# Queries in 1 KB runs, turned on VectorE, with scores on 32-row tiles and gates on GpSimd

## The chip, the cores and the metric

The kernel runs on one core of one Trainium2 chip. The metric is the device time of one execution in microseconds. Below, PE is the matrix engine TensorE, PEld its weight loads, DVE is VectorE, ACT is ScalarE, POOL is GpSimd, and SP is the engine that here issues the stores.

## The reference, cut to what matters

The inputs `q`, `k` and `v` have the shape (8 batches, 8 heads, 576 tokens, 64). A first attention pools keys and values by 8 to 72 of each. Its output, 512 features per token, goes into four experts, each a causal attention with 64-wide heads; a gate picks two of the four per token.

```python
k_p = k.reshape(B, H, Sp, pool, D).mean(axis=3)          # pool = 8, Sp = 72; v_p the same
scores = scale * np.matmul(q, k_p.transpose(0, 1, 3, 2))
attn = softmax(scores);  x = (attn @ v_p), heads side by side   # (8, 576, 512)
...
logits = x @ w_gate                                       # 4 experts
topk, w = the two largest of logits, softmax over these two
for e in range(E):
    q, k, v = x @ wq[e], x @ wk[e], x @ wv[e]
    a = softmax(scale * q @ k.T, causal)
    out += (w of e where e is picked) * (a @ v @ wo[e])
```

## The kernel before, in words

All work of a batch b is cut into small steps, and one long string `SEQ` (L551) gives the order of the steps of all batches, written out by hand. Each token names a step, its batch, for products the PSUM bank, and by a trailing d that DVE, not ACT, evacuates it. A trailing c sets `cut`, so that `wide` splits a product of 128 output rows into four of 32. PE, ACT, DVE and POOL each run their instructions in this order. SP's stores follow the order of the program among themselves.

Loads: `load` (L109) issues the tokens `L_q`, `L_k` and `L_v` on POOL, as DMAs that turn float32 into bf16. A batch's queries come in six loads of 96 tokens, with one token to a partition, so each run in memory is one head's 64 numbers, 256 B. Keys and values come in three loads each with two tokens to a partition. There are three raw buffers of each kind (`NRAW`). `load_weights` (tokens `W`) issues the weights on POOL too, and `order_weights` (tokens `c`) copies them into the order that the products need.

The first attention: `PK` and `PV` pool keys and values by products with a constant matrix; `kc` and `vc` evacuate them. `KT` transposes the pooled keys on PE (four flips, 96 columns each, one per pair of heads), `kt` evacuates them into `kpT`. `Q` transposes the queries of a pair of heads on PE (six flips) and `r` evacuates them into `qT`. `Es` computes the scores, with the 72 pooled keys padded to 96 output rows: for each of four pairs of heads two products of 512 columns, which lie in different 64-row tiles of PE, and for the last 64 tokens (`E4`) two products of 64 columns per pair. `es` takes the exponential on ACT, out of two banks at a time. `Dn` sums the exponentials by products, `dn` and `dx` form the reciprocal by a logarithm and an exponential on ACT, `Ov` multiplies by the values, and `ov` normalises on DVE into `xT`.

The experts: `P` projects queries and keys (`p` evacuates into `qk`), `V` projects values and gate logits (`v`). `Sb` and `sb` compute scores and exponentials (`etb`); `am` masks the diagonal blocks on POOL (`a`). `gate` is done in ten small steps per batch: g0 an exponential on ACT, and on DVE g1 to g3 the second largest logit by maxima and minima (five operations), g4 the mask, g5 to g9 the two weights. `Bv` multiplies by the values; `bv` normalises in three steps: `bz` a reciprocal on DVE, `bg` its product with the gate on DVE, `b` the scaling into `osc` on DVE. `T` and `t` transpose into `oT`; `Y`, `y` and `z` apply the last weight and store the output, from eight buffers `ofin`. At the start and wherever data are late, `warm_up` (tokens `H`) issues products that nobody reads, 51 in all.

Copies run through one helper (L176), products through `mm` (L185), transposes through `flip` (L194), so many rows of the profile share a line and are told apart by their tiles.

Of the kernel before, what the change touches and what calls it, by code (L numbers as in the profile page):

```python
# [12 lines left out]
MINOP = mybir.AluOpType.min  # L13
MAXOP = mybir.AluOpType.max
ISGE = mybir.AluOpType.is_ge
ISLE = mybir.AluOpType.is_le
ISEQ = mybir.AluOpType.is_equal
# [4 lines left out]
def kernel(  # L22
# [34 lines left out]
    NQC = S // KR  # L57
# [16 lines left out]
    qraws = bufs(NRAW, [KR, NQC, H, D], BF16, "qraw")  # L74
    kraws = bufs(NRAW, [KR, 3, H, 2, D], BF16, "kraw")
    vraws = bufs(NRAW, [KR, 3, H, 2, D], BF16, "vraw")
    kps = bufs(2, [KR, H * D], BF16, "kp")
    kpTs = bufs(2, [128, NHP, KR], BF16, "kpT")
    vps = bufs(2, [KR, H, D], BF16, "vp")
    qTs = bufs(8, [128, S], BF16, "qT")  # L80
    etas = bufs(2, [KR, NHP, 2, S], BF16, "eta")
# [24 lines left out]
    wst = {nm: const.tile([128, E, 2, 2, HD], BF16, name=f"wst_{nm}") for nm in ("q", "k", "v")}  # L106
    wst_g = const.tile([128, 2, 2, E], BF16, name="wst_g")

    def load(b, nm, c):  # L109
        if nm == "q":  # L110
            dst = qraws[b % NRAW][:, c, :, :]
            src = q[b, :, KR * c : KR * (c + 1), :].rearrange("h p d -> p h d")
        else:
            raw, T = (kraws, k) if nm == "k" else (vraws, v)
            dst = raw[b % NRAW][:, c, :, :, :].rearrange("p h t d -> p h (t d)")
            src = T[b, :, 2 * KR * c : 2 * KR * (c + 1), :].rearrange("h (p t) d -> p h (t d)", t=2)
        nc.gpsimd.dma_start(out=dst, in_=src)  # L117


    def load_weights(i):  # L120
        if i < 3:
            dst = wst["qkv"[i]][:].rearrange("p e g t d -> p (e g) (t d)")
# [9 lines left out]
    def order_weights(i, dve):  # L132
# [4 lines left out]
        else:  # L137
            copy(dve, wvg[:, :, 0 : E * HD].rearrange("p fc (e d) -> p fc e d", e=E),
                 wst["v"][:].rearrange("p e g t d -> p (g t) e d"))
            copy(dve, wvg[:, :, E * HD : VG], wst_g[:].rearrange("p g t e -> p (g t) e"))  # L140

    def setup_consts(step):
# [9 lines left out]
        else:  # L152
# [5 lines left out]
            nc.vector.tensor_scalar_mul(out=poolv[:], in0=poolk[:], scalar1=DSC)  # L158

# [56 lines left out]
    def pool_pe(b, bank, raw, mat):  # L216
        for t in range(2):
            for c in range(3):
                mm(psum[32 * c : 32 * c + 32, bank, :], mat[:, :], raw[:, c, :, t, :],
                   start=(t == 0), stop=(t == 1))  # L220

    def PK(b, bank):
        pool_pe(b, bank, kraws[b % NRAW], poolk)

    def kc(b, bank, dve):
        copy(dve, kps[b % 2][:], psum[0:KR, bank, :])

    def PV(b, bank):
        pool_pe(b, bank, vraws[b % NRAW], poolv)
# [7 lines left out]
    def KT(b, bank):  # L237
        for hp in range(NHP):
            flip(half_bank(bank)[:, KR * hp : KR * hp + KR],
                 kps[b % 2][:, 128 * hp : 128 * hp + 128])  # L240

    def kt(b, bank, dve):
        copy(dve, kpTs[b % 2][:],
             half_bank(bank)[:, 0 : NHP * KR].rearrange("p (a n) -> p a n", a=NHP))

    def Q(b, bank, hp):
        for c in range(NQC):
            flip(half_bank(bank)[:, KR * c : KR * (c + 1)],
                 qraws[b % NRAW][:, c, 2 * hp : 2 * hp + 2, :].rearrange("p h d -> p (h d)"))

    def r(b, bank, dve, hp):
        copy(dve, qTs[4 * (b % 2) + hp][:], half_bank(bank)[:, 0:S])


    def Es(b, bank, hp):
        for i in range(NHP) if hp == NHP else [hp]:
            c0, n, at_ = (MAIN, TAIL, TAIL * i) if hp == NHP else (0, MAIN, 0)
            for hh in range(2):
                r0 = hh * D
                mm(psum[0:KR, bank + hh, at_ : at_ + n], kpTs[b % 2][r0 : r0 + D, i, :],  # L260
                   qTs[4 * (b % 2) + i][r0 : r0 + D, c0 : c0 + n])

    def es(b, bank, dve, hp):
        eta = etas[b % 2]
        if hp == NHP:
            for hh in range(2):
                nc.scalar.activation(
                    out=eta[:, :, hh, MAIN:S],
                    in_=psum[0:KR, bank + hh, 0 : NHP * TAIL].rearrange("p (a n) -> p a n", a=NHP),
                    func=EXP, scale=ATT_EXP_SCALE,  # L270
                )
        else:
            nc.scalar.activation(  # L273
                out=eta[:, hp, :, 0:MAIN], in_=psum[0:KR, bank : bank + 2, :],
# [3 lines left out]
    def heads(b, g, cols):  # L278
        for i in range(4):
            yield i, 4 * g + i, etas[b % 2][:, 2 * g + i // 2, i % 2, cols]  # L280

# [9 lines left out]

    def dn(b, bank, dve, g):
# [6 lines left out]

# [36 lines left out]
    def gate(b, step):  # L336
# [14 lines left out]
        elif step == 1:  # L351
            L2 = L.rearrange("p c (a b) -> p c a b", b=2)
            for nm, op in (("hi", MAXOP), ("lo", MINOP)):
                nc.vector.tensor_tensor(
                    out=tmp(nm, 2, 1), in0=L2[:, :, :, 0:1], in1=L2[:, :, :, 1:2], op=op
                )
        elif step == 2:
            for nm, src, op in (("s2", "hi", MINOP), ("s3", "lo", MAXOP)):
                nc.vector.tensor_tensor(
                    out=tmp(nm, 1), in0=got(src)[:, :, 0, :], in1=got(src)[:, :, 1, :], op=op  # L360
                )
        elif step == 3:
            nc.vector.tensor_tensor(
                out=tmp("m2", 1), in0=got("s2"), in1=got("s3"), op=MAXOP
            )
        elif step == 4:
            nc.vector.tensor_tensor(
                out=tmp("msk", E), in0=L, in1=got("m2").to_broadcast([128, n, E]), op=ISGE
            )
        elif step == 5:  # L370
            nc.vector.tensor_mul(out=tmp("W", E), in0=got("Ex"), in1=got("msk"))
        elif step == 6:
            nc.vector.tensor_add(
# [9 lines left out]
        else:  # L383
            nc.vector.tensor_mul(
# [91 lines left out]
    def bv(b, bank, step, ep, part):  # L476
# [6 lines left out]
        elif step == "bg":  # L483
            nc.vector.tensor_mul(
# [220 lines left out]
```

The softmax here doesn't subtract the row's maximum and nothing guards it: scores larger than these inputs give would overflow.

## Time and profile before

| What | Value |
|---|---|
| Median of 3 runs | 167.1 us (166.84 to 168.86) |
| Span of the profiled execution, first to last instruction | 165.0 us |
| Time of the profiled execution itself | not given apart from its span |
| Mean granted clock of PE | 0.996 |
| First product of an expert projection | 26.23 us |
| Last copy of an output ends, last stores are issued | 161.15 us, 161.22 us |
| Query transposes on PE | 192 |
| Loads of queries, keys, values | 48, 24, 24 |
| DMA packets, and those under 512 B | 84204, 79312 |

The page gives the span and the busy time of each engine. Groups of instructions have the line, the engine, the operation, the tiles by name (output, then inputs), the shape, the count, the busy time and the mean length of one. The timeline has the start and the length of each instruction or run of like instructions, and in brackets the idle time of the engine before it with what ended that. A product is pipelined: its length holds a passage through the array that overlaps the next product, so what it costs is read from start to start. The mean costs that the steps below meet most often are these:

| Group | Count | Mean of one |
|---|---|---|
| ACT exponential of scores, 96x1024 from PSUM | 32 | 1.02 us |
| ACT exponential of tail scores, 96x256 | 16 | 0.38 us |
| DVE copy of turned queries, 128x576 bf16 | 24 | 0.45 us |
| ACT copy of turned queries | 8 | 0.64 us |
| POOL issue of a query load | 48 | 0.78 us |
| DVE copy of an output or a projection, 128x512 | 46 | 0.69 us |
| ACT copy of an output, 128x512 | 18 | 0.59 us |
| DVE small operations of gate and `bg` | 108 | 0.18 us |

### The profile page before, as it was taken

To read this page: it belongs to the slowest core of one execution; us is meant where nothing else is said; L and a number is where in the kernel's file an instruction comes from. 1 tells how busy PE (TensorE), PEld (TensorE's weight loads), DVE (VectorE), ACT (ScalarE), POOL (GpSimd) and SP (SyncE) were. 2 spreads that over 40 slices of the span, in tenths; PEclk is the share of its full clock that TensorE was granted. 3 is DMA by queue.
4 is the path that set the end of the run, shared out by engine and by line. 5 is a ranking of instruction groups with operands and counts; after the bars stand their busy time and mean duration, and the time that the engine had idled before them with its cause. 6 is when DMAs were issued, how large, how long until landed. Compare 5 with 4: busy or idle time off the path is not lost. (4 is left out here: it accounts for less than half of the span.)

```text
span 165.0 us, 6106 instructions
## 1 busy us (share of the span) xinstructions
PE 157.0 (95%) x2463; PEld 93.8 (57%) x2463; DVE 123.8 (75%) x410; ACT 135.0 (82%) x247; POOL 104.9 (64%) x178
## 2 busy tenths in 40 slices
PE   6999988999999999999999999999999999999980
PEld 2344354568557656654754878555647686555730
DVE  1101497589799859976988899998998989779960
ACT  3029758999998999888998997789997999898860
POOL 6999891899999999965959997400140211364100
PEclk9999999999999999999999999999999999999998
DMA  2999999999999999999999999923113043055875
GB/s 22 160 153 171 164 172 178 170 145 139 177 156 173 164 157 148 156 233 217 206 178 226 168 198 83 174 100 86 47 68 127 4 131 127 0 190 195 257 260 191
DMA packets 84204, 25.04 MB, mean 152 GB/s; under 512 B 79312, under 2 KB 79568, under 8 KB 84176
## 3 DMA queue, kind: packets, MB, share of 16 engines
q0 software_dynamic: 78928, 15.21, 110.6%
q1 hardware_dynamic: 5024, 9.05, 15.9%
q8 instruction: 19, 0.31, 0.7%
q10 hardware_dynamic: 224, 0.39, 0.6%
q14 instruction: 9, 0.07, 0.1%
HBM read 30.42 MB, written 9.44 MB: 242 GB/s over the span
## 5 line engine op out<-in xcount | busy, mean ns | idle before, releaser
L433 ACT ACTIVATE etb_97<-psum 128x1024 bf16<-128x1024 f32 x24 | 23.6, 1023 | 2.5 <-PE psum L185 2.4
L433 ACT ACTIVATE etb_98<-psum 128x1024 bf16<-128x1024 f32 x24 | 23.5, 1027 | 1.3 <-PE psum L185 1.1
L450 POOL TENSOR_SCALAR_AFFINE_SELECT etb_98<-etb_98 128x256 bf16<-128x256 bf16 x32 | 12.5, 410 | 17.4 <-ACT etb_98 L433 17.2
L450 POOL TENSOR_SCALAR_AFFINE_SELECT etb_97<-etb_97 128x256 bf16<-128x256 bf16 x32 | 12.4, 415 | 15.8 <-ACT etb_97 L433 15.7
L173 PE MATMUL psum<-warm 128*128 128x512 bf16 x51 | 15.2, 443 | 1.8 <-DVE onesd L146 1.3
L273 ACT ACTIVATE eta_91<-psum 96x1024 bf16<-96x1024 f32 x16 | 15.9, 1018 | 1.1 <-PE psum L185 1.1
L273 ACT ACTIVATE eta_92<-psum 96x1024 bf16<-96x1024 f32 x16 | 15.6, 1020 | 0.7 <-PE psum L185 0.6
L117 POOL DMA_DIRECT2D qraw_68<-in_q_dram x18 | 13.9, 775 | 1.2 <-PE psum L185 1.1
L176 DVE COPY ofin<-psum 128x512 f32<-128x512 f32 (+1 forms) x18 | 11.9, 673 | 3.2 <-PE psum L185 2.4
L117 POOL DMA_DIRECT2D qraw_69<-in_q_dram x18 | 13.8, 770 | 0.5 <-issue 0.5
L176 DVE CAST qk_99<-psum 128x512 bf16<-128x512 f32 (+1 forms) x16 | 10.5, 670 | 3.8 <-PE psum L185 3.6
L176 DVE CAST qk_100<-psum 128x512 bf16<-128x512 f32 (+1 forms) x16 | 10.5, 654 | 3.5 <-PE psum L185 3.5
L176 ACT COPY ofin<-psum 128x512 f32<-128x512 f32 (+1 forms) x19 | 10.7, 580 | 2.7 <-PE psum L185 1.8
L185 PE MATMUL psum<-wvg,xT_96 128*32 128x260 bf16 (+1 forms) x120 | 10.8, 275 | 0.0
L173 PEld LDWEIGHTS <-warm 128*128 128x128 bf16 x51 | 5.1, 111 | 9.5 <-issue 5.8
L185 PE MATMUL psum<-wvg,xT_95 128*32 128x260 bf16 (+1 forms) x156 | 10.5, 275 | 0.0
L185 PEld LDWEIGHTS <-etb_97 128*128 128x128 bf16 x240 | 8.8, 97 | 2.0 <-issue 0.4
L117 POOL DMA_DIRECT2D qraw_70<-in_q_dram x12 | 9.2, 784 | 0.0
L185 PEld LDWEIGHTS <-etb_98 128*128 128x128 bf16 x240 | 8.3, 97 | 1.4 <-issue 0.8
L185 PE MATMUL psum<-qk_100 64*128 64x64 bf16 (+4 forms) x96 | 8.8, 276 | 0.1
L117 POOL DMA_DIRECT2D kraw_71<-in_k_dram x9 | 7.0, 787 | 2.7 <-DMA qraw_70<-in_q_dram 1.8
L185 PE MATMUL psum<-qk_99 64*128 64x64 bf16 (+4 forms) x96 | 8.4, 277 | 0.0
(198 smaller groups left out, 452.8 us busy)
## 6 DMA issues: line engine op xcount, KB each, us to landing
out_dram<-ofin SPq DMA_DIRECT2D x31, 256.0 KB, 3.0
kraw_71<-in_k_dram POOLq DMA_DIRECT2D x9, 192.0 KB, 6.2
qraw_68<-in_q_dram POOLq DMA_DIRECT2D x18, 96.0 KB, 5.3
vraw_74<-in_v_dram POOLq DMA_DIRECT2D x9, 192.0 KB, 5.5
kraw_72<-in_k_dram POOLq DMA_DIRECT2D x9, 192.0 KB, 5.9
qraw_69<-in_q_dram POOLq DMA_DIRECT2D x18, 96.0 KB, 5.5
vraw_75<-in_v_dram POOLq DMA_DIRECT2D x9, 192.0 KB, 4.9
kraw_73<-in_k_dram POOLq DMA_DIRECT2D x6, 192.0 KB, 6.5
```

Source lines behind the costliest of these rows:

```text
L117: nc.gpsimd.dma_start(out=dst, in_=src)
L173: nc.tensor.matmul(out=psum[:, bank, :], lhsT=warm[:, 0:128], rhs=warm[:], start=True, stop=True)
L176: (nc.vector.tensor_copy if dve else nc.scalar.copy)(out=out, in_=in_)
L185: nc.tensor.matmul(out=out, lhsT=lhsT, rhs=rhs, start=start, stop=stop)
L273: nc.scalar.activation(out=eta[:, hp, :, 0:MAIN], in_=psum[0:KR, bank : bank + 2, :], func=EXP, scale=ATT_EXP_SCALE,)
L433: nc.scalar.activation(out=et[:, ep, :, eo : eo + n], in_=psum[:, bank : bank + 2, 0:n], func=EXP, scale=MOE_EXP_SCALE,)
L450: nc.gpsimd.affine_select(out=blk, in_=blk, pattern=[[0, 2], [1, 128]], compare_op=ISGE, fill=0.0, base=0, channel_multiplier=-1,)
```

## The change

Queries. The first 512 tokens of a batch come in two loads, each of four heads, with four neighbouring tokens to a partition (runs of 1 KB). The last 64 tokens of four batches share one tile `qtl`, 32 partitions to each batch, with two tokens to a partition (tokens `L_t`). Nothing of the queries is transposed on PE any more. `turn` (tokens `U`) is a DVE transpose of 32x32 blocks of 32-bit words, that is of pairs of bf16 numbers, from SBUF to SBUF: two for each batch and one for the tails of four batches. Partition 32r+x of `qT` then holds numbers 2x and 2x+1 of the tokens of row group r.

Scores. A head's 64 numbers are summed in two products of 32 rows each (t = 0 and 1), every second number of a partition. Four row groups, each with 128 of the tokens, run on four 32-row tiles into four banks; the tail of batch b lies in row group b%4 alone. As the same keys must stand in every row group, `kpT` holds four rotated copies. Batches 0 and 1 (`TURNED`) make them with 16 flips on PE and a second copy `kd` of the pooled keys; the other batches make one on PE, and six SBUF to SBUF copies issued by SP (tokens `R`) make the others. PK reads its input with a stride of two numbers. A call of `Es` covers four heads; `es` reads two of the four banks with a stride of 32 floats and writes in the order of the tokens, and takes the tails with one activation.

Gates. The picked experts are found by comparing all pairs of logits on POOL; g1 to g6 and g9 move to POOL, and so does `bg`.

The rest. The weights' staging tiles lie in `oT`. `SEQ` is written anew throughout. The evacuations on DVE fall from 32 to 29 for `p`, from 22 to 21 for `v`, from 17 to 15 for `y` and from 21 to 17 for `t`, the others of each going to ACT; those of `kt` rise from 3 of 8 to 9 of 10. The warm-up products are 42.

```diff
-    qraws = bufs(NRAW, [KR, NQC, H, D], BF16, "qraw")
+    qraws = bufs(NRAW, [128, H, QT, D], BF16, "qraw")
+    qtls = bufs(B // QUAD, [128, H, 2, D], BF16, "qtl")
+    qTts = bufs(B // QUAD, [128, H, 2, 32, 2], BF16, "qTt")
...
-    kpTs = bufs(2, [128, NHP, KR], BF16, "kpT")
+    kpTs = bufs(2, [128, NRG, NHP, KR], BF16, "kpT")
...
         if nm == "q":
-            dst = qraws[b % NRAW][:, c, :, :]
-            src = q[b, :, KR * c : KR * (c + 1), :].rearrange("h p d -> p h d")
+            hs = slice(NHP * c, NHP * c + NHP)
+            dst = qraws[b % NRAW][:, hs].rearrange("p h t d -> p h (t d)")
+            src = q[b, hs, 0:MAIN, :].rearrange("h (p t) d -> p h (t d)", t=QT)
+        elif nm == "t":
+            dst = qtls[b // QUAD][32 * c : 32 * c + 32].rearrange("p h t d -> p h (t d)")
+            src = q[b + c, :, MAIN:S, :].rearrange("h (p t) d -> p h (t d)", t=2)
...
     def KT(b, bank):
-        for hp in range(NHP):
-            flip(half_bank(bank)[:, KR * hp : KR * hp + KR],
-                 kps[b % 2][:, 128 * hp : 128 * hp + 128])
...
+        for i in range(NRG if b in TURNED else 1):
+            for hp in range(NHP):
+                c = 32 * (-i % NRG)
+                o = KR * (NHP * (i % 2) + hp)
+                flip(half_bank(bank + i // 2)[:, o : o + KR], kps[b % 2][:, hp, c : c + 128])
...
-    def Q(b, bank, hp):
-        for c in range(NQC):
-            flip(half_bank(bank)[:, KR * c : KR * (c + 1)],
-                 qraws[b % NRAW][:, c, 2 * hp : 2 * hp + 2, :].rearrange("p h d -> p (h d)"))
...
+    def spread(b):
+        for k in range(1, NRG):
+            n = 32 * (NRG - k)
+            for d0, s0, m in ((32 * k, 0, n), (0, n, 128 - n)):
+                nc.sync.dma_start(out=kpTs[b % 2][d0 : d0 + m, k], in_=kpTs[b % 2][s0 : s0 + m, 0])
...
+        nc.vector.transpose(out=dst.rearrange("p h s x t -> p (h s x t)").bitcast(U32),
+                            in_=src.rearrange("p h s d -> p (h s d)").bitcast(U32))
...
+        def score(r, h, t, out, qT):
+            rows = slice(32 * r, 32 * r + 32)
+            nc.tensor.matmul(
+                out=out, lhsT=kpTs[b % 2][rows, (r - 2 * (h % 2) - t) % NRG, h // 2, :],
+                rhs=qT[rows, h, :, :, t].rearrange("p s x -> p (s x)"),
+                start=(t == 0), stop=(t == 1), tile_position=(32 * r, 0),
+            )
...
+                if u == NHP:
+                    score(b % QUAD, h, t, psum[0:KR, bank, TAIL * h : TAIL * h + TAIL], qTts[b // QUAD])
+                else:
+                    o = 128 * (h % NHP)
+                    for r in range(NRG):
+                        score(r, h, t, psum[0:KR, bank + r, o : o + 128], qTs[b % 2])
...
+            nc.scalar.activation(
+                out=etas[b % 2][:, NHP * u : NHP * u + NHP, 128 * r : 128 * (r + n)].rearrange(
+                    "j h (r p t) -> j r h p t", r=n, t=QT),
+                in_=psum[0:KR, bank + r : bank + r + n, :].rearrange("j r (h t p) -> j r h p t", h=NHP, t=QT),
+                func=EXP, scale=ATT_EXP_SCALE,
+            )
...
         elif step == 1:
...
+            nc.gpsimd.tensor_sub(
+                out=tmp("Df", E, E), in0=L.unsqueeze(3).to_broadcast([128, n, E, E]),
+                in1=L.unsqueeze(2).to_broadcast([128, n, E, E]),
+            )
         elif step == 2:
...
+            nc.gpsimd.tensor_scalar(out=got("Df"), in0=got("Df"), scalar1=0.0, scalar2=None, op0=ISLT)
         elif step == 3:
...
         elif step == "bg":
-            nc.vector.tensor_mul(
+            nc.gpsimd.tensor_mul(
...
-        I:0 L_k0:0 L_k1:0 L_k2:0 J:0 K:0 H19:0@0 PK:0@0 kc:0 H4:0@1 KT:0@0 kt:0 L_q0:0 L_q1:0
-        L_q2:0 L_q3:0 L_q4:0 L_q5:0 H8:0@1 Q2:0@0 r2:0 Q1:0@1 Q3:0@2 r1:0d r3:0 H1:0@3 E2:0@4
...
-        bz02:7 Y2:7@1 bg02:7 bg12:7 y3:7 b02:7 y2:7p Y0:7@0 z2:7 y0:7 Y1:7@2 b12:7 T12:7@4
-        t12:7d y1:7 t12:6d T02:7@6 t02:7d Y4:7@6 ya4:7 yb4:7d
+        I:0 J:0 K:0 L_k2:0 L_k1:0 L_k0:0 H14:0@7 PK:0@7 L_t1:0 kd:0d kc:0 H4:0@6 KT:0@5 kt1:0 L_q1:0
+        L_k1:1 L_t0:0 U1:0 kt0:0d H5:0@7 E1:0@1 e11:0 M:0 L_t3:0 L_t2:0 U2:0 L_q0:0 e10:0 H4:0@7
+        E4:0@0 H3:0@7 D1:0@5 e4:0 L_k2:1 L_k0:1 U0:0 E0:0@1 e00:0 PK:1@7 kd:1d L_v2:0 L_v1:0 L_v0:0
+        D2:0@0 kc:1 H5:0@6 KT:1@6 L_q1:1 d2:0 L_k1:2 e01:0 H1:0@0 D0:0@4 PV:0@2 L_k2:2 kt0:1d x2:0
+        d0:0 d1:0 kt1:1d E4:1@6 e4:1 x1:0 vc:0d H1:0@7 O10:0@7 U1:1 L_k0:2 H1:0@5 E1:1@2 e10:1
+        O11:0@6 O01:0@1 o11:0 o10:0 O00:0@0 W0:0 L_q0:1 x0:0 o01:0 o00:0 D2:1@6 W1:0 PK:2@7 kc:2
...
+        b02:7 Y0:7@2 y0:6 bz01:7 bg12:7 y0:7 b12:7 T12:7@4 bg01:7 T02:7@5 bz11:7 bg11:7 t12:7d
+        t02:7d Y1:7@0 b11:7 y1:7 Y4:7@4 ya4:7 T11:7@6 t11:7 b01:7 T01:7@1 yb4:7d t01:7d Y3:7@2 y3:7
+        Y2:7@3 y2:7d
```

## The prediction

> **What bounds the kernel now.** I read the page's busy shares first, then the busy times by stretch, then the timeline at three places. A busy PE is not a full PE, so a share proves little; only the distance from start to start shows what a product occupies.
>
> ```profile
> PE 157.0 (95%) x2463; PEld 93.8 (57%) x2463; DVE 123.8 (75%) x410; ACT 135.0 (82%) x247; POOL 104.9 (64%) x178
> ```
>
> The stretch from 30 to 160 us, in the view of busy time by stretch (columns: PE, weight loads, DVE, ACT, POOL, clock, DMA, GB/s):
>
> ```profile
> 30.00:160.00 130.00, 129.10 (x2214) 81.37 (x2206) 112.66 (x374) 117.45 (x217) 80.47 (x142) 1.00 1.20 151
> ```
>
> PE stands idle for 0.9 of 130 us at a clock of 1.00; ACT is idle for 12.5, DVE for 17.3. The list of waits has no wait of PE on a compute engine longer than 1.3 us in total. So behind 30 us PE sets the pace, with ACT close behind. The timeline of PE shows what occupies it:
>
> ```profile
> 23.48 1.19 PE L194 MATMUL psum<-ident,qraw_69 96*128 96x96 bf16 x24
> ...
> 28.60 0.21 PE L185 MATMUL psum<-qT_87,kpT_80 64*96 64x64 bf16 x2
> 28.65 0.21 PE L185 MATMUL psum<-qT_88,kpT_80 64*96 64x64 bf16 x2
> 28.69 0.21 PE L185 MATMUL psum<-qT_89,kpT_80 64*96 64x64 bf16 x2
> 28.74 0.21 PE L185 MATMUL psum<-qT_90,kpT_80 64*96 64x64 bf16 x2
> 28.78 0.40 PE L185 MATMUL psum<-qT_89,kpT_80 64*96 64x512 bf16 x2
> 29.11 1.05 PE L185 MATMUL psum<-xT_95,wkp_123 128*32 128x512 bf16 x16
> ```
>
> The columns are start and length in us. 24 query transposes take 1.19 us, (1.19-0.21)/23 = 43 ns each. Pairs of 64-column score products, two row tiles at a time, follow every 45 ns, though 64 columns stream in less. 16 products of 512 columns on four tiles take 1.05 us: (1.05-0.38)/3 = 0.22 us per four, so four tiles run at once. At a change of tile shape (28.78 to 29.11) a pass of 0.22 takes 0.33, so a change costs 0.11.
>
> Ahead of 26 us another chain rules:
>
> ```profile
> 18.25 0.90 POOL L130 DMA_DIRECT2D wst_q<-in_moe_wq_dram  x1
> 24.46 0.62 ACT L176 COPY wqp_120<-wst_q 128x512 bf16<-128x512 bf16 x1 [1.18 <-DMA wst_q<-in_moe_wq_dram]
> 26.23 1.15 PE L185 MATMUL psum<-xT_95,wqp_120 128*128 128x512 bf16 x8
> ```
>
> The first expert projection runs at 26.23, after a weight that POOL issues at 18.25 behind 21 input loads, and after batch 0's last `xT` (DVE at 24.31). Until then PE fills with warm-up products.
>
> [...] no run here shows an ACT read with a large stride.
>
> **The change, part by part.**
>
> Query transposes. 192 products and 32 evacuations go. From 26.23 us on, six batches remain: 6 x 1.19 = -7.1 us of PE. The first two lie in the start.
>
> Scores. Per batch 4 pairs of 512 columns (4 x 0.22 = 0.88) become 16 fours of 128 columns, at 0.22/4 = 55 ns each 0.88. No run here shows four row tiles; two row tiles and four column tiles do run at once, so I take it, and the bound is fours that run two by two, +0.88 x 6 = 5.3. Calls fall from four to two: -2 x 0.11 = -0.2, over six batches -1.2; batch 1's remainder after the first projection (0.46 for 0.22) gives 0.2 back: -1.0.
>
> Tail scores. Batch b's queries 512 to 575 lie in rows 32(b%4) alone, so 16 products of 64 columns run one after another: 16 x 45 ns = 0.72 against 4 x 45 = 0.18 per batch. Before has seven behind the first projection, after has six: 4.3 - 1.3 = +3.0. Lower bound 16 x 29 ns (the spacing of attention-value products at the end of the trace, six 65-column ones in 0.34 us), +1.5. Upper bound: weight loads that overlap nothing, 16 x 0.12 by their length of 119 ns, +10; the pairs above, on the same tiles again and again, exclude it nearly.
>
> Rotated keys. For batches 0 and 1 KT does 16 flips, +12 x 43 ns each, in the start, in place of warm-ups: nothing, and 1.0 us if that cover is gone. For the others six SP copies per batch: SP's first store comes at 66.03 us, so early ones meet an empty queue. At later ones the stores wait behind R, 6 x about 0.5 us of issue (SP's last store issues in 0.47) plus R's wait for `kt`. Eight output buffers cover that; uncovered, 3 us of delay per batch before its scores, on PE.
>
> DVE. Gone: 24 query copies x 0.45 = 10.8; 72 small gate operations x 0.18 = 13.1; 36 gate products x 0.18 = 6.5. Added: 18 turns of 512 words. [...] Key copies +3.6; projections, stores and transposes moved to ACT -5.8. Net -19.8: DVE 104, and 117 at the upper bound. Not a limit.
>
> ACT. Gone: 8 query copies x 0.64 = 5.1; 16 tail exponentials of 0.38 become 8 of about 0.6, -1.2; key copies -1.6. Added: three projections, two stores, one value copy, four `oT`, about +5.5. Net -2.4. The 32 large exponentials (1.02 each) now read PSUM at a stride of 32 floats. I take 1.02; bounds 1.02 and twice.
>
> POOL and DMA. 48 query loads x 0.777 = 37.3 become 16 x 0.78 and 8 tails at about 0.5: -20.8. Added: 64 gate operations and 36 products. Nearest rows: `affine_select` of 256 elements 0.41, `iota` of 128 0.25; I take 0.25, 25 us (bounds 0.1 and 0.6). POOL stays near 109. In each normalisation DVE's next product now waits for POOL. What stands in POOL's queue there are masks waiting for ACT (8.6 us at the longest) and loads waiting for buffers; DVE's spare time hides it, 0.25 x 36 = 9 us if it did not. Query runs grow from 256 B to 1 KB, so fewer packets; DMA holds PE for 0.5 us in all now, little to gain.
>
> Start. Ahead of the first weight load 21 loads of 0.78 become 19, four of them tails: 16.4 falls to about 13.7, -2.7, and `wst_q` lands near 21.8. Batch 0's first scores need one half of the queries: that half is issued second behind the keys, not last of six. Keys are copied by about 10, KT ends near 10.5, copies by 11.4, first scores 11.4 for 13.14, so -1.7. But ACT then serves two exponentials of batch 1 before batch 0's last normaliser. The later chain decides: I take -2.0 (bounds -3 and +1).
>
> End. Before closes with an output cut in halves: 0.42 us copy, 128 KB landing in 2.3 to 2.6. After closes with two whole ones: 0.22 us more of PE, 0.69 for 0.42 of copy, 256 KB landing in 3.0: +1.0.
>
> Sum against the profiled span of 165.0: -7.1 - 1.0 + 3.0 - 2.0 + 1.0 = -6.1, a span of 158.9. The median shown, 167.1, is 2.1 above that span; carried over, 161.0.
>
> **Rivals.** (1) ACT takes over. PE loses 5.1 us behind the first projection, ACT only 2.4 of 117 in that stretch, and needs order as well. If ACT keeps its idle share, behind the start only 2.4 x 130/117 = 2.7 is won, the end takes 1.0, and with a start of -1.0 the time is 167.1 - 2.7 = 164.4. For it: ACT 90% busy in that stretch. Against it: 12.5 us idle there, and the gain asks for 2.7 of them.
>
> (2) Slower, by POOL in the normalisations: `bz` on DVE, `bg` on POOL, `b` on DVE. DVE will have 17.3 + 19.8 = 37 us to spare, so it decides once `bg` comes on average more than 37/36 = 1.0 us late; at 1.35 us, 36 x 0.35 = 12.6 eats the gain of 6.1 and adds 6.5: 173.6. For it: POOL's queue is in order and now holds waits for ACT. Against it: masks of later tiles are mostly ready, behind the start the waits that POOL ends sum to 0.2 us in the list.
>
> (3) Slower, by strided PSUM reads of the exponentials. It cancels the gain once each is 6.1/32 = 0.19 us longer; at twice the cost 32 x 0.85 + 8 x 0.43 = 31 us fall on ACT, which has 12.5 + 2.4 free: 161 + 16 = 177, or more. [...]
>
> **How the numbers follow.** My forecast 0.55, own range 157 to 163.7; (1) 0.2, around 164.4 and within 2%; (2) 0.15; (3) 0.1. The 2% on either side, 163.8 and 170.4, is about what a measurement of this kernel can tell from no change. So faster 0.55, same 0.2, slower 0.25. Predicted 161.0. The range 156.5 to 175 leaves out about 0.05 below (tail products at 29 ns and a start of -3 give 158.5, a better order more) and 0.12 above, the worse parts of (2) and (3).
>
> **What would show it.** Right: no `ident,qraw` products; fours of 128 columns every 55 ns; tail products every 45 ns; the first projection near 24 us; exponentials of 96x1024 still at 1.02; turns near 0.7; PE without idle time behind it. Wrong: exponentials above 1.2; `osc` products with long waits on POOL; PE idle for several us behind its first projection; scores waiting for a rotated `kpT`.

## The result: slower by 8 per cent

The kernel after takes 182.3 us (180.0 to 183.2, 4 runs), the kernel before 167.0 beside it. The ratio is 1.079, 95% interval 1.071 to 1.087. The forecast was 161.0, with 175 as its upper end. The profiled execution (183.1 us, a span of 181.4 at a mean clock of 0.939) is one of two that ran over 1.5% longer than the fastest, and as the ratios here and below leave such runs out (here they rest on spans of 178.3 and 179.8 us, at 0.955 and 0.960), sizes read from it are somewhat too large.

The page of the kernel after, its busy times and its row of the granted clock in 40 slices of 4.5 us:

```profile
PE 163.0 (90%) x3158; PEld 97.1 (54%) x3158; DVE 110.9 (61%) x293; ACT 135.1 (74%) x238; POOL 108.4 (60%) x254
...
PEclk9957997899999997559999999999999999999998
```

PE's share fell from 95% to 90%, and the clock, which before was full nearly throughout (a mean of 0.996), falls to 0.50 near 12, 30 and 70 to 80 us. The busy times by stretch show where (columns: PE, weight loads, DVE, ACT, POOL, clock, DMA, GB/s), first after, then before:

```profile
30.00:80.00 50.00, 43.69 (x919) 24.37 (x919) 29.66 (x67) 37.27 (x67) 35.47 (x66) 0.88 1.52 171
80.00:165.00 85.00, 84.56 (x1825) 54.59 (x1823) 61.43 (x160) 75.59 (x136) 45.27 (x135) 1.00 0.58 114
```

```profile
30.00:80.00 50.00, 49.95 (x893) 31.10 (x886) 41.23 (x125) 46.19 (x87) 46.07 (x71) 1.00 1.83 170
80.00:160.00 80.00, 79.15 (x1326) 50.27 (x1323) 71.43 (x249) 71.26 (x131) 34.40 (x72) 1.00 0.81 139
```

From 80 us on both kernels keep PE busy. The loss lies between 30 and 80 us: there PE stands idle for 6.3 us where before it was 0.05, and the mean clock of 0.88 costs up to 0.12 x 50 = 6.0 more. The start adds 4.0, since the first expert projection runs at 30.2 us, before at 26.23. That is 16.3 us. The forecast had -5.1 for PE's work behind the start and +1.0 for the end; the sum of 12.2 leaves 4.2 of the 16.4 us between the spans without a place. PE's own list of waits, which before had nothing above 1.3 us, now names:

```profile
PE psum L199 <- DVE qk L190: 4.1, 2, 3.1
PE psum L199 <- DMA kraw<-in_k_dram: 3.3, 1, 3.3
PE psum L199 <- issue: 2.1, 2, 1.7
```

The columns are the wait in us in total, the number of times, the longest. The priced operations themselves came out close to their estimates. Exponentials, and turns of the queries, in the groups of instructions (busy us, mean ns), and the tail's products in PE's timeline:

```profile
L311 ACT ACTIVATE eta<-psum 96x1024 bf16<-96x1024 f32 x32 | 31.5, 1016 | 3.3 <-PE psum L286 3.3
...
L280 DVE STREAM_TRANSPOSE qT<-qraw 128x512 uint32<-128x512 uint32 x16 | 11.0, 693 | 0.2 <-DMA qraw<-in_q_dram 0.2
```

```profile
82.19 0.81 PE L286 MATMUL psum<-qTt,kpT 32*96 32x64 bf16 x14
```

The exponential still takes 1.016 us out of PSUM at a stride of 32 floats (1.02 before, without it), a turn 0.69 us. 14 tail products from first to last start are about (0.81-0.21)/13 = 46 ns each, a pass being 0.21.

### The profile page after: what moved, and what is told of

It is laid out like the page before. It is cut to its first block, busy times and chain, and to the rows that moved or that the text cites. A ratio compares the mean times of both kernels' runs of the same rounds, so it can differ in the third digit from the quotient of the medians.

```text
span 181.4 us, 7497 instructions
## 1 busy us (share of the span) xinstructions
PE 163.0 (90%) x3158; PEld 97.1 (54%) x3158; DVE 110.9 (61%) x293; ACT 135.1 (74%) x238; POOL 108.4 (60%) x254
## 4 chain that ended last, share of the span: by engine, by line
PE 81%; POOL 6%; DMA 4%; issue 3%; ACT 1%; DVE 1%; ACTq 1%; POOLq 0%; DVEq 0%
PE psum L199 64%; PE psum L286 8%; PE psum L208 5%; PE psum L187 4%; DMA kraw<-in_k_dram 4%; POOL kraw L130 2%; POOL etb L488 1%; ACTq L578 1%; ACT kp L190 1%; POOL qraw L130 1%; ACT ofin L190 1%; DVE xT L356 0%; POOL Df L396 0%; DVE qk L190 0%; DVE kp L190 0%
## 5 line engine op out<-in xcount | busy, mean ns | idle before, releaser
L471 ACT ACTIVATE etb<-psum 128x1024 bf16<-128x1024 f32 x48 | 47.9, 1025 | 7.2 <-PE psum L199 6.5
L311 ACT ACTIVATE eta<-psum 96x1024 bf16<-96x1024 f32 x32 | 31.5, 1016 | 3.3 <-PE psum L286 3.3
L488 POOL TENSOR_SCALAR_AFFINE_SELECT etb<-etb 128x256 bf16<-128x256 bf16 x64 | 24.9, 408 | 10.1 <-ACT etb L471 10.1
L130 POOL DMA_DIRECT2D kraw<-in_k_dram x24 | 19.0, 793 | 8.7 <-DMA kraw<-in_k_dram 2.5
L356 DVE TENSOR_TENSOR xT<-psum,rza 128x512 bf16<-128x512 f32 x32 | 21.1, 685 | 3.7 <-PE psum L199 3.0
L199 PE MATMUL psum<-xT,wkp 128*32 128x512 bf16 (+3 forms) x332 | 21.4, 291 | 2.1 <-issue 2.1
L199 PE MATMUL psum<-wvg,xT 128*32 128x260 bf16 (+1 forms) x444 | 23.1, 280 | 0.0
L199 PE MATMUL psum<-xT,wqp 128*32 128x512 bf16 (+3 forms) x320 | 21.2, 304 | 0.0
L199 PE MATMUL psum<-wop,oT 128*128 128x512 bf16 (+2 forms) x92 | 20.2, 375 | 0.4 <-ACT oT L190 0.4
L199 PE MATMUL psum<-vaug,etb 128*128 128x65 bf16 x480 | 20.0, 197 | 0.0
L190 DVE COPY ofin<-psum 128x512 f32<-128x512 f32 (+1 forms) x16 | 10.6, 669 | 7.7 <-ACT ofin L190 3.1
```

The source lines that it names most:

```text
L190: (nc.vector.tensor_copy if dve else nc.scalar.copy)(out=out, in_=in_)
L199: nc.tensor.matmul(out=out, lhsT=lhsT, rhs=rhs, start=start, stop=stop)
L311: nc.scalar.activation(out=etas[b % 2][:, NHP * u : NHP * u + NHP, 128 * r : 128 * (r + n)].rearrange("j h (r p t) -> j r h p t", r=n, t=Q ...
L356: nc.vector.tensor_tensor(out=xT[:, 2 * g + t, mcols(b)], in0=psum[:, bank, :], in1=rz[:, g, 0:MAIN], op=MULT)
L471: nc.scalar.activation(out=et[:, ep, :, eo : eo + n], in_=psum[:, bank : bank + 2, 0:n], func=EXP, scale=MOE_EXP_SCALE,)
L488: nc.gpsimd.affine_select(out=blk, in_=blk, pattern=[[0, 2], [1, 128]], compare_op=ISGE, fill=0.0, base=0, channel_multiplier=-1,)
```

## The experiments

Three causes stood at first: PE's idle stretches at the start and the half clock behind them; the gates on POOL, for which DVE waits, and PE for DVE; and loads in POOL's queue ahead of masks and gates. A fourth came out of the traces: stops of PE at one place in the count of its own instructions. Each row compares with runs of the kernel before on the same chip; between rows the ratio is the measure, since the kernel before itself took from 167.0 to 168.2 us.

| Kernel | Median us | Before beside it | Ratio (95%) |
|---|---|---|---|
| after, idle PE filled | 181.7 | 168.1 | 1.084 (1.079 to 1.088) |
| after, gates on DVE | 178.0 | 168.1 | 1.059 (1.051 to 1.067) |
| after, eight loads late | 178.9 | 168.1 | 1.066 (1.062 to 1.069) |
| after, gates and bg on DVE | 176.5 | 168.2 | 1.048 (1.043 to 1.053) |
| ... and filled | 179.0 | 168.2 | 1.064 (1.057 to 1.070) |
| ... filled, 17 projections whole | 179.8 | 168.2 | 1.071 (1.064 to 1.078) |
| gates and bg on DVE, loads late | 177.4 | 167.1 | 1.060 (1.055 to 1.065) |
| ... and 17 projections whole | 176.2 | 167.1 | 1.055 (1.049 to 1.060) |
| ... and start filled | 177.1 | 167.5 | 1.055 (1.046 to 1.063) |
| ... and all 49 divided products whole | 176.7 | 167.5 | 1.053 (1.046 to 1.059) |
| before, gates and bg on POOL | 194.1 (189.9 to 196.1) | 168.1 | 1.155 by medians, 1.134 by the lowest |
| before, gates alone on POOL | 191.0 | 167.1 | 1.139 (1.131 to 1.148) |
| before, bg alone on POOL | 173.4 | 167.1 | 1.038 (1.032 to 1.044) |
| before, 51 projections divided | 178.8 | 168.2 | 1.059 (1.053 to 1.066) |
| before, 14 warm-ups for 19 | 167.4 | 167.5 | 1.000 (0.998 to 1.002) |

### Idle PE filled with warm-ups

```diff
-H14:0@7 ... O00:0@0 ... PV:4@6
+H29:0@7 ... H6:0@0 O00:0@0 ... H12:0@6 PV:4@6
```

> The changed kernel with more warm-up products where PE stood idle (15 more ahead of the first pooling of keys, 6 ahead of batch 0's second-half attention values, 12 ahead of batch 4's pooling of values), nothing else. Theory 1 (idle PE halves its own clock for 3 to 11 us after each of three stretches, 10 us of clock in all, and that half-speed work is on the path): the clock stays near 1.00 and the time falls by 5 to 9 us from about 181.5, to 172.5 to 176.5. Rival (the work after each stretch waits for data anyway, the slow clock only fills waiting): the clock rises but the time stays within 2 us of 181.5.

181.7 us: nothing gained, though the mean clock rose to 0.977. So the half clock at the start falls as a cause of the total. The later fall stayed (the clock is 1.00 on average up to 60.4 us, 0.93 from 30 to 80), so this run says nothing on that one. DVE's list of waits says where the gain went:

```profile
DVE den L415 <- POOL d L411: 9.7, 2, 6.6
```

In the kernel after this sum was 7.9 with a longest of 4.9. DVE had done its work at 60.1 us in place of 63.2 and then waited longer: POOL ended `d` at 66.7 in place of 68.1.

### The gates on DVE, and the loads behind them

The gate's steps g1 to g6 and g9 get the text of the kernel before; `bg` stays on POOL.

> The changed kernel with the gate's steps g1 to g6 and g9 back on DVE as before (maxima and minima), the products bg still on POOL, the order of all tokens unchanged. Theory 2 (the gate's steps stand in POOL's queue behind loads that wait for a DMA to land, DVE's next gate step then holds DVE's queue for 4.9 and 3.0 us, and PE idles for a projection that DVE has not evacuated): these two waits vanish, PE's 3.1 and 1.1 us of idle time near 66 and 73 us with them, and the half clock from 70 to 81 us too: 6 to 10 us less than 181.5. Rival (POOL is not what is late there; DVE and PE would have waited for data anyway): less than 3 us gained.

178.0 us, a ratio of 1.059 for 1.079: the gates on POOL do cost time, but some 3 us and not the 6 to 10 expected. The other side of the same queue are eight loads that stood ahead of the masks:

```diff
-L_t0:4 ... L_t2:4 ... L_t3:4 ... L_t1:4 ... L_k2:6 ... L_k0:6 ... L_k1:6 ... L_q0:5 ... g9:0
+g9:0 L_t0:4 L_t2:4 L_t3:4 L_t1:4 L_k2:6 L_k0:6 L_k1:6 L_q0:5
```

> The changed kernel with eight loads that nobody needs soon (the tails of batches 4 to 7, keys of batch 6, one half of batch 5's queries) moved in POOL's queue from between the gate's steps of batch 0 and 1 to behind the last of batch 0; gates stay on POOL. Theory 2 by its first half (loads in POOL's queue make the gates late): DVE's wait for the gate's sum falls from 7.9 us to under 4, 2 to 6 us gained on 181.5. Rival (POOL's own gate operations and masks are what takes long): DVE's wait stays above 6 us and the time within 1.5 us.

178.9 us (1.066), so the loads in the queue count too, for some 2 us; DVE's wait for `d` fell from 7.9 to 5.4 us, between the two expectations. How the two act together is seen in the kernel after, in DVE's timeline and POOL's over the same time:

```profile
62.52 0.70 DVE L280 STREAM_TRANSPOSE qT<-qraw 128x512 uint32<-128x512 uint32 x1
68.10 0.16 DVE L415 SCALAR_TENSOR_TENSOR den<-d 128x4 f32<-128x4 f32 x1 [4.88 <-POOL d L411]
...
68.39 0.99 DVE L190 CAST qk<-psum 128x512 bf16<-128x512 f32 x2
72.40 0.17 DVE L415 SCALAR_TENSOR_TENSOR den<-d 128x5 f32<-128x5 f32 x1 [3.02 <-POOL d L411]
```

```profile
62.82 0.40 POOL L396 TENSOR_SCALAR Df<-Df 128x64 f32<-128x64 f32 x1
63.16 1.85 POOL L488 TENSOR_SCALAR_AFFINE_SELECT etb<-etb 128x256 bf16<-128x256 bf16 x5
65.00 0.31 POOL L391 TENSOR_TENSOR Df<-L 128x80 f32<-128x80 f32 x1
...
66.98 0.85 POOL L130 DMA_DIRECT2D kraw<-in_k_dram  x1 [0.52 <-issue]
67.85 0.21 POOL L411 TENSOR_TENSOR d<-W 128x8 f32<-128x8 f32 x1
```

DVE works at 62.5 us, then stands 4.88 us for the one small operation `d` on POOL, then once more 3.02. In POOL's queue five masks (1.85 us), the gate of the other batch pair (65.00) and a load (66.98) stood ahead of `d` (67.85). Behind DVE's waiting `den` was the copy of `qk` (68.39), for which PE's next product waited:

```profile
69.43 0.40 PE L199 MATMUL psum<-eta,onesd 96*32 96x512 bf16 x4 [3.08 <-DVE qk L190]
```

### bg on DVE as well

```diff
-            nc.gpsimd.tensor_mul(
+            nc.vector.tensor_mul(
                 out=gt[:, :, :, 0], in0=rz[:, :, :, 0],
```

> The kernel after with g1 to g6, g9 and bg all back on DVE in the forms of before, so that DVE never waits for POOL in the gates; everything else as after. If what was left of the loss in the kernel with the gates alone on DVE (178.0 us) is mostly DVE's wait for bg behind loads and masks in POOL's queue (1.7 us of PE idle at 66.8 us there, and the half clock that followed to 72 us, about 1.5 us more), this runs near 175. If that wait only covers another one (products waiting for instructions, or for ACT), it stays at 177 to 179. PE should still stop about 2 us near 47 us and again near 60 us, each with no releaser in the profile.

176.5 us, between the two expectations. The whole move of small operations to POOL costs the kernel after about 5 us (ratio 1.079 to 1.048, about 3% of 167). That leaves over half of the loss. The stop expected near 47 us is there, with what follows it:

```profile
48.00:50.00 2.00, 0.36 (x6) 0.00 (x0) 0.14 (x2) 1.00 (x3) 1.39 (x3) 1.00 1.58 193
50.00:52.00 2.00, 1.81 (x25) 0.76 (x28) 0.86 (x2) 0.81 (x1) 1.21 (x2) 0.74 1.67 202
52.00:54.00 2.00, 2.00 (x34) 1.15 (x28) 1.61 (x4) 0.66 (x3) 1.11 (x2) 0.50 1.72 195
```

PE does nothing for 1.6 of the 2 us from 48 to 50 and then has a clock of 0.74 and 0.50.

> The same kernel (gates and bg on DVE) with 33 more warm-up products at the three places of the start where PE stood idle. On the kernel after alone these moved the time by under 1 us. If that was because POOL's chain of loads and gates then set the time near 70 us, then without that chain the fill brings its 2 to 3 us here: 172 to 173.5. If the clock at the start does not matter at all, it equals the kernel without the fill (within 1 us).

179.0 us, slower by 2.5, against both expectations. The kernel after had waited where the 12 warm-ups ahead of `PV:4` stand; now that wait was gone, and they kept PE from other work, from 64.96 us on for 2.75 us. The other 21 brought nothing in a later kernel either ("start filled").

### PE's stops without a releaser

The kernel after has stops on PE that no engine or DMA ends ("issue"). PE's timeline:

```profile
50.52 1.04 PE L199 MATMUL psum<-xT,wkp 128*32 128x512 bf16 x13
53.25 0.38 PE L199 MATMUL psum<-xT,wkp 128*32 128x512 bf16 x1 [1.68 <-issue]
```

Counting PE's products and weight loads up to a stop, in the busy times from 0 to that moment (PE's count, then the loads' count, in brackets), in the kernel after and in the filled one:

```profile
0.00:51.20 51.20, 45.06 (x735) 22.90 (x736) 25.04 (x60) 31.08 (x52) 36.98 (x54) 0.90 1.57 169
0.00:63.90 63.90, 56.08 (x991) 29.49 (x992) 33.08 (x79) 41.23 (x71) 45.13 (x69) 0.92 1.59 173
```

```profile
0.00:46.72 46.72, 43.90 (x735) 22.41 (x736) 24.68 (x59) 30.39 (x51) 34.45 (x50) 1.00 1.57 169
0.00:60.40 60.40, 55.24 (x991) 29.08 (x992) 33.46 (x79) 41.07 (x69) 43.30 (x64) 1.00 1.60 174
```

735 + 736 = 1471 and 991 + 992 = 1983, in both kernels, though the fill shifted the products and the stop therefore came ahead of another one (the list of waits puts the second of the filled kernel down to ACT). 1471 = 5 x 256 + 191 and 1983 = 7 x 256 + 191; the stop at 108.0 us comes at 3775 = 14 x 256 + 191. The page has a queue of the kind "instruction" (columns: packets, MB, share of 16 engines), in the kernel after and in the one before:

```profile
q8 instruction: 24, 0.39, 0.9%
```

```profile
q8 instruction: 19, 0.31, 0.7%
```

These are packets of 16 KB, 24 for 6316 of PE's products and weight loads and 19 for 4926, so one for about 260. Ahead of the first stop of the kernel after a packet starts at 51.0 us and ends at 51.9, and PE goes on at 53.25. At its three stops at this place of the count (1.68, 0.48 and 0.40 us long) PE goes on 1.40 to 1.45 us behind the end of such a packet. In the kernel before, which has no such stop, PE comes to the same places of the count 1.28 us or more behind it. The theory was then that the stops are waits for the next 256 instructions. To test it, 17 divided projections ahead of 70 us were made whole:

```diff
-P_q1:0@1c P_q0:0@7c V1:0@4c V0:0@0c V2:0@3c V3:0@4c P_k1:1@4c P_t0:1@7c ...
+P_q1:0@1 P_q0:0@7 V1:0@4 V0:0@0 V2:0@3 V3:0@4 P_k1:1@4 P_t0:1@7 ...
```

> The same again (gates and bg on DVE, fill), and 17 projections of batches 0 to 2 undivided: one product of 128 output rows where four of 32 stood. The arithmetic is the same, PE gets 552 instructions fewer ahead of 70 us, and pays up to 0.2 us per call for changes of tile shape (at most 3.4 us, some save one). Theory: PE's stops without a releaser, always at one and the same count of PE instructions modulo 256, are waits for the fetch of the next 256 instructions, because short products use up the fetched ones faster than the next come in a time when the DMA engines are full. Then the two stops (2.4 and 1.7 us) go or shrink below 0.5 us each, and the time falls by 1 to 4 us against the kernel with gates on DVE and fill. Rival: the stops are waits on data that the profile does not show (a DMA, a buffer); then they stay at the same products, and the time rises by the changes of shape.

The early stop, of 2.5 us in the filled kernel, went. The time did not fall (179.8): PE now stood elsewhere, two times for masks on POOL, and once more without a releaser behind 100 us:

```profile
PE psum L201 <- POOL etb L491: 1.7, 2, 0.9
PE psum L288 <- issue: 1.1, 1, 1.1
```

The reverse edit gives the kernel before more instructions for the same work:

```diff
-P_q0:0@0 P_k0:0@1 V3:1@6 V0:1@0 V2:1@7 ...
+P_q0:0@0c P_k0:0@1c V3:1@6c V0:1@0c V2:1@7c ...
```

> The kernel before with 51 more projections (all of P_q, P_k and V that were whole) divided into four products of 32 output rows; nothing else is changed. PE's work in columns is the same, its instructions grow by 1224 or more, to about the number of the kernel after. By the theory of the instruction fetch, stops of 1 to 2.5 us appear on PE without a releaser, at the same count modulo 256 as in the kernel after, above all between 30 and 75 us where the DMA engines are full, and the time rises by 2 to 6 us, to 169 to 173. By the rival the number of instructions costs nothing: no such stops, and 166.5 to 168.5 with the changes of shape that fall away or are added.

178.8 us, more than the theory expected. The stops appeared, behind 31.2, 70.8 and 88.8 us, at the same place in the count: 351 + 352 = 703 = 2 x 256 + 191, 1631 + 1632 = 3263 = 12 x 256 + 191, and 2494, one less than 9 x 256 + 191, at 70.8 us. PE's list of waits and the counts:

```profile
PE psum L185 <- issue: 4.9, 3, 2.3
```

```profile
0.00:31.26 31.26, 27.53 (x351) 12.75 (x352) 11.07 (x36) 17.33 (x29) 25.21 (x38) 1.00 1.73 148
0.00:88.79 88.79, 82.53 (x1631) 46.71 (x1632) 55.73 (x168) 66.89 (x121) 75.05 (x114) 1.00 1.73 158
```

So more instructions for the same columns bring stops of up to 2.3 us at this place of the count, as the theory of the fetch has it. The other half of the 10.6 us is not in these stops. Counted in the trace, neighbouring products of different tile shape rise from 185 to 223. From start to start, without the stops, the projections behind the first one took 53.6 us for 49.4.

### What is left without POOL's gates

> The kernel after with gates and bg on DVE (176.5 us), and eight loads of batches 4 to 6 (four query tails, three keys, one query half), which stood in POOL's queue ahead of the masks of batches 0 and 1, moved behind g9 of batch 0. With gates and bg off POOL nothing that DVE waits for stands behind loads any more; what remains there is masks, which PE's products with the values wait for. If these were late, the time falls to 174 to 176; if the loads no longer matter, it stays within 1 us of 176.5. The stop of 2 us without a releaser near 47 us stays, at the 1471st PE instruction, because the count of instructions is the same.

177.4 us, within 1 us of 176.5. By the ratios, which allow for the chip, it is 1.060 for 1.048, and the intervals do not touch. So late loads gain nothing once DVE waits for nothing behind them, and seem to cost some 2 us; why was not tried. The stop without a releaser stayed, 1.8 us long.

> The same with the 17 projections of batches 0 to 2 undivided (552 PE instructions fewer ahead of 70 us), and without added warm-up products. In the kernel with the fill the two stops went, but PE then stood 2 us near 61 us for masks behind loads in POOL's queue, and 12 added warm-up products ran in a stretch where PE had work. With the loads late and no fill these two are out of the way: if the fetch of instructions is the largest cause that is left, the stop of 2 us and the half clock behind it (1.7 us) go, and the time is 171 to 173.5. If the gain is only handed to the next wait, it is 175.5 to 178, as with the fill.

176.2 us, the second case: without the large early stops it is 1.2 us better, and within the intervals the same (1.055 for 1.060). The gain is handed to the next wait.

> The kernel after with gates and bg on DVE, the eight loads late and 17 projections whole (176.2 us), with 29 warm-up products in place of 14 ahead of the first keys and 6 more ahead of batch 0's products O00, but without the 12 that stood in PE's way at 65 us. If idle PE and the half clock at the start (10 to 14 and 28 to 32 us there, some 3 us lost against the kernel before at 32 us) are what is left, the time falls to 172.5 to 174.5. If other chains (loads, DVE) set the start, it stays at 175.5 to 177.

177.1 us, a ratio of 1.055 as without the fill: no gain, though the clock of the profiled execution is 0.996. The idle start and the clock are not what is left.

> The same as the last, with all 49 divided projections whole, those behind 70 us too. Theory of the fetch: behind 70 us its stops are small (0.3 to 1.3 us each, some 2 us in all), so at most 2 us are won, and up to 64 more changes of tile shape at 0.1 us each are paid: the time is within 3 us of the last kernel, either way. If instructions are costly everywhere it falls by over 3 us, to below 170.5.

176.7 us: the same within the intervals, as the fetch theory allowed. Its trace has no such stop of 0.3 us or more any longer, so these stops are not what is left either.

> The kernel before with 14 warm-up products ahead of the first keys in place of 19, as the kernel after has them; nothing else. PE then waits about 1.9 us, from 6.3 to 8.2, for the first keys. If this idle stretch alone halves the clock for several us and delays the start, the time rises by 1 to 4 us, to 168 to 171. If the chain of loads sets the start anyway (the first weight lands at 24.4), the time stays within 0.8 us of 167.

167.4 us, no change. There PE's wait for the first keys was 0.6 us and the clock stayed at 1.00 from 6 to 14 us; in the profiled run of the kernel after it was 3.27, partly because `PK` begins with chunk 0, which is now loaded last of three (argued from the order of the tokens, not tried).

### Parts of the change in the old order

The gate steps, and then each part alone, were put on POOL in the kernel before.

> The kernel before with this one part of the change alone: gate steps g1 to g6, g9 and the products bg on POOL, all tokens in their old places. If POOL's queue makes gates late in any order (theory 2): over 3 us slower than 167.0, with DVE waiting for POOL. If it is only the new order of loads: within 2 us of 167.0.

> The kernel before with g1 to g6 and g9 on POOL in the forms of after, and bg on DVE, in the old order. Theory: POOL takes its queue in order, and a gate that waits up to 9 us for its logits holds every load and mask behind it, so that PE waits for raw queries and values. Then most of the 26 us of the kernel with both on POOL is here: 183 to 192. If instead bg was the larger part, this stays at 168 to 174.

> The kernel before with bg alone on POOL (24 full and 12 shorter products of about 0.2 us), in the old order; gates stay on DVE. In the kernel before with gates and bg on POOL DVE waited 9.7 us for bg and 22.9 us of POOL's time went to waits for the gates' inputs. If bg is the smaller part, as by the second rival in the prediction at a small delay, the time is 168 to 172. If the chain of bz, bg and b alone costs what that rival priced, it is 174 to 180.

194.1, 191.0 and 173.4 us; the last lies between its two expectations. With gates alone, POOL waits for logits at the head of its queue, and PE for the loads that stand behind:

```profile
POOL Df L353 <- DVE L L177: 12.4, 3, 11.1
```

```profile
PE psum L186 <- DMA vraw<-in_v_dram: 4.4, 4, 1.5
PE psum L195 <- DMA qraw<-in_q_dram: 4.1, 6, 1.2
```

Beside three waits of POOL of 12.4 us in total PE waits 8.5 us for values and queries. With bg alone DVE waits little but often, 11 times, and the time rises by 3.8% (3.2 to 4.4):

```profile
DVE osc L489 <- POOL gt L484: 6.3, 11, 1.8
```

The gates on POOL cost 14% in the old order and 2% in the new one (1.079 for 1.059), so the new order serves them far better.

## Why the prediction was wrong

**Right.** Query transposes are gone. In 9 of 16 score calls of 32 products the last product starts 0.45 us after the first, 58 ns a four (forecast 55). Tail products come every 46 ns (forecast 45). Weight loads were 121 ns long for 96 columns (`kpT`), 100 for 128 (`etb`) and 97 for 32 (`xT`), so their lengths do not follow the columns. Exponentials and turns took what was forecast (above); for the turns no run of before showed a price, so near 0.7 us and their share in the net for DVE were the author's estimate. POOL was busy for 108.4 us (forecast 109), ACT for 135.1 (132.6). Rival 3 fell on the exponentials' 1.016 us. No product waited for rotated keys in PE's list of waits. DVE was busy for 110.9 us (104, the turns 12.4 of it), and no limit.

**Wrong: "DVE's spare time hides it."** The step for POOL priced the small operations rightly (0.19 to 0.41 us, for 0.25) and looked only at `bg`. It named masks and loads in POOL's queue, but not `den`, which waits on DVE for a gate step behind them, and what stands behind `den` on DVE: the copies PE needs. The spare 37 us were a sum over the run; the waits of 4.9 and 3.0 us came within 10 us of each other. This is rival 2's kind of mechanism at another instruction. In the kernel after, `osc` waited only 1.9 us for `bg` in all. Moving the operations back shows its cost: about 5 us.

**Wrong: the start, -2.0.** The step let POOL's issue of 19 for 21 loads set the landing of `wst_q` at 21.8. It landed at 26.7. The 19 loads are fewer but larger: 3328 KB for 2880. POOL stood 1.6 us for an earlier load to land and issued the weight (into `oT`, where it is now staged) at 17.62, for 18.25 before, and it was 9.1 us under way, for 6.2. So the step counted issues alone; the bytes rose by 448 KB, and the landing came 2.2 us later. In the profiled run even this weight did not come last:

```profile
10.15 1.55 POOL L130 DMA_DIRECT2D kraw<-in_k_dram  x2 [1.59 <-DMA kraw<-in_k_dram]
17.62 0.88 POOL L142 DMA_DIRECT2D oT<-in_moe_wq_dram  x1
```

```profile
26.92 2.48 DVE L356 TENSOR_TENSOR xT<-psum,rza 128x512 bf16<-128x512 f32 x4 [1.50 <-PE psum L199]
29.32 0.28 DVE L190 COPY wqp<-oT 128x512 bf16<-128x512 bf16 x1
```

```profile
29.58 0.48 PE L208 MATMUL psum<-ident,kp 96*128 96x96 bf16 x4 [0.68 <-ACT kp L190]
...
30.20 1.90 PE L199 MATMUL psum<-xT,wqp 128*32 128x512 bf16 x16
```

DVE copied the weight at 29.32, behind four products for `xT`, and PE waited for ACT's pooled keys until 29.58. The first projection ran at 30.2 us there, and at 26.3 to 30.2 in the variants. Refilling the start did not move the total, so this term alone was not the cause.

**Missing: the clock.** The sum held PE's speed constant. In the kernel after the clock fell to 0.50 at 9.2, 29.6 and 70.6 us, for 6.8, 3.4 and 10.2 us. The first fall came in an idle stretch of 3.3 us, the third behind one of 3.1; near the second PE was idle for 1.5 of 4 us and never over 0.7 at once. With gates and bg on DVE it fell to 0.50 behind a stop of 1.8 us, and in the filled form of that kernel behind one of 2.5. It stayed at 1.00 behind a stop of 1.86 us with only the gates on DVE, and around stops of up to 2.3 us with the divided projections in the old order. So the runs show no length of idle time that decides it. With the gates on POOL PE was idle for 6.3 us and lost up to 6.0 by the clock; as the fill gained nothing, how much of the 6.0 lay on the path is not shown.

**Missing: PE's instructions.** The sum counted columns and not instructions. PE's products rose from 2463 to 3158. Stops without a releaser, 2.6 us in PE's list of waits, came with it.

**Mis-sized: the scores, and what the new order does to other products.** With gates and bg on DVE, loads late, 17 projections whole and the start filled, the ratio is still 1.055, and the clock of its profiled execution was full nearly throughout (0.996). Its busy times by stretch:

```profile
30.00:80.00 50.00, 47.40 (x884) 27.70 (x882) 39.70 (x106) 45.06 (x81) 37.27 (x62) 1.00 1.66 193
80.00:165.00 85.00, 81.74 (x1701) 53.37 (x1706) 67.68 (x253) 72.67 (x132) 25.16 (x59) 1.00 0.54 129
```

PE is idle for 2.6 us and 3.3 us there, and the span is 8.0 above that of before. Counted in both traces, behind the first projection and from the start of one product on PE to the start of the next (idle time above 0.28 us apart, as stops), the forecast's terms came out so:

| Term, us | Before | This kernel | Difference | Forecast |
|---|---|---|---|---|
| First projection starts | 26.2 | 27.3 | +1.0 | -2.0 |
| Query transposes | 6.6 | 0 | -6.6 | -7.1 |
| Scores without tails | 6.8 | 8.7 | +1.9 | -1.0 |
| Tail scores | 1.6 | 4.0 | +2.4 | +3.0 |
| Projections | 49.4 | 50.8 | +1.4 | 0 |
| Scores and values of the experts | 29.1 | 31.0 | +1.9 | 0 |
| Sums and values of the first attention | 12.1 | 14.0 | +1.9 | 0 |
| Stops | 0.7 | 4.3 | +3.6 | 0 |
| All other products | 28.2 | 27.5 | -0.6 | 0 |
| Behind the last product | 4.4 | 5.4 | +1.0 | +1.0 |
| Sum | | | +8.0 | -6.1 |

The step for the scores failed by 2.9 us: a call of 32 products took 0.67 us up to the next product (forecast 0.55), a pair in the kernel before 0.27 (forecast 0.33). The prediction had read the 0.11 us of a change of tile shape at one place; for the pairs that was too much, for the calls too little. In six kernels of the new order these scores took 8.3 to 8.8 us. The terms put at nothing came to 8.2 us. Behind the five stops of this kernel stand a mask on POOL (1.3), `qk` on DVE (0.7), `oT` on ACT (0.4), and twice nothing but "issue" (0.8 and 1.1).

**Open.** No run tells which part of the new order makes the other products longer or the stops, and the queries' change was not tried in the old order. No later kernel has a lower ratio than the one with gates and bg on DVE alone, 1.048. Some PE records are missing in some of the traces, so such sums are good to some tenths of a us.

## What to carry to other kernels

Before small operations are moved to an engine whose queue also issues loads, follow one of them through that queue: who waits for its result, on which engine, and what stands behind the waiting instruction there. Spare time in total says nothing about that. When loads are made fewer and larger, count their bytes and not only their issues (19 loads for 21 were 448 KB more here, and the weight behind them landed 2.2 us later). Count PE's instructions as well as its columns when products are divided, and read the cost of a change of tile shape at more than one place. An idle PE was followed by the half clock in some places (behind 3.1 us, for 10.2 us) and not in others (behind 1.86 us); whether that costs anything was not clear here.

## What the runs showed of the hardware

PE stopped for 0.4 to 2.3 us at counts of its products and weight loads of 190 or 191 modulo 256: three times in the kernel after, twice each in its filled form and with the gates on DVE, at 48 us with gates and bg on DVE, and three times in the kernel before with 51 projections divided. In the kernel after it went on 1.40 to 1.45 us behind the end of a 16 KB packet of the instruction queue. The granted clock went to 0.50 behind stops of 1.8 and 2.5 us in two kernels and stayed at 1.00 around stops of 1.86 and 2.3 us in two others. An exponential on ACT of 96x1024 out of PSUM took 1.016 us at a stride of 32 floats in the kernel after, and 1.018 to 1.020 without it in the kernel before. A DVE transpose of 128x512 words took 0.69 us. In the kernel after, small POOL operations of 2 to 80 numbers per partition took 0.19 to 0.41 us, the means of each shape, where an `affine_select` of 256 took 0.41.
